# Windowed attention with two feed-forward layers on one core: one polynomial step gets a choice of engine, and the order of all work is found anew

## The chip, the core and the metric

The kernel runs on one core of a Trainium2 chip. The metric is the time of one execution on the device in microseconds. Before the change it was run three times, with a median of 931.73 us (930.45 to 932.07).

A core has engines that work at the same time, each through its own queue and strictly in that queue's order: TensorE (PE) multiplies matrices, VectorE (DVE) and GpSimd (POOL) do elementwise work, ScalarE (ACT) computes `func(scale * x + bias)`, and SyncE (SP) issues the DMAs. An engine whose next instruction waits does nothing else in the meantime. Results of TensorE lie in PSUM, everything else in SBUF.

## What is computed

Three stages run one after the other. Everything is float32.

```python
scores = scale * np.matmul(q, k.transpose(0, 1, 3, 2))      # 4 batches, 8 heads, 576 positions, 64 wide
scores = np.where(mask, scores + bias[None], -1000000000.0)  # window of 128, slopes by head
attn = softmax(scores);  x = np.matmul(attn, v)              # then 2304 tokens x 512

h = x @ w_in                                                 # layer 1: 512 -> 2048
P = a[0] + a[1]*h + a[2]*h*h + a[3]*h*h*h
Q = 1.0 + np.abs(b[0])*np.abs(h) + np.abs(b[1])*h*h
x = (P / (Q + 1e-06)) @ w_out                                # 2048 -> 512

r = np.maximum(x @ w2_in, 0.0)                               # layer 2: 512 -> 2048
out = (r * r) @ w2_out                                       # 2048 -> 512
```

The denominator Q is evaluated by Horner's scheme from `ah = |h|`: the first step is `t = |b1| * ah + |b0|`, the second `t = t * ah`, and the 1 is added in the logarithm that follows.

## The kernel before

**Stages and tiles.** Attention works on 16 pairs of heads. Layer 1 runs over five blocks of tokens, numbered 0 to 4 (512 tokens each, block 1 has 256). In a block there are 16 steps `f`, one for each 128 of the 2048 hidden columns. A step first computes `h` with 12 matmuls (`gemm_in`, L758; the planner's name is `g1`), then passes `h` through a chain on the other engines, and then adds its part to the block's output with 12 more matmuls (`gemm_out`, L843, `g2`). Each operand is split into a high and a low half (`xh`/`xl`, `gh`/`gl`, weights `hi`/`lo`), and three products are summed. Layer 2 runs over blocks 5 to 8 of 512 tokens in two pairs, and a last block 9 of 256. In the pairs the first product is done by Strassen's scheme: block 5 or 7 computes for each of eight `r` the products m1, m2, m6, m7 and m4 (L907, 6 matmuls each), with a `g2` before m7 and one before m4 once the first `r` is through. Blocks 6 and 8 reuse saved products and need only m5 and m3. Block 9 is computed plainly.

**The chain of a step in layer 1.** `r_abs` (ACT, L771) makes `ah`; `r_u` (ACT, L775) and `r_p` 1 and 2 (DVE, L791 and L793) make the numerator; `r_t` 1 (POOL, L783) and `r_t` 2 (POOL, L785) make the denominator; `r_r` 1 and 2 (ACT, L799 and L801, a logarithm and an exponential) its reciprocal; `r_g` 1 to 3 (DVE, L811) a correction of it and the quotient. Then `gh` (ACT, L230) and `gl` (DVE, L237) split the result for `g2`. There are four PSUM banks for `h`, so `g1` of a step waits until `gl` of the step four before it is done.

**Work beside the chain.** The weights come as float64 in 64 chunks of 512 KB (`wl`, L207) and are turned to float32 on the chip: `w0` (ACT, POOL or DVE), `w1`, `w2`, `w3` (DVE, L222, L224, L226), `w4` (ACT or POOL) and `w5` (POOL or DVE, L237). For Strassen's scheme sums of the second layer's weights (`wS`, L251, then `sh` and `sl`) are made while layer 1 runs, written to DRAM, and read back as `wc` (`wcl`, L887, six buffers). Sums of the layer's input are made as well (`xrraw`, L866, then `xh` and `xl`). In blocks 5 and 7 the products m1, m6, m7 and m4 all leave the same PSUM bank one after the other, so each is copied away first (`keep`, L333 on ACT and L335 on DVE; the planner's names are c1, c6, c7 and c4): m6 waits for c1, m7 for c6, m4 for c7.

**What sets the order.** All work is entered in a `Plan` with its predecessors, the engines that may do it, a duration for each, and a priority. The priority is the place in the computation plus a constant for the kind of work from the table `BIAS`. `Plan.run` then goes through the work while the program is built: among everything whose predecessors are placed it takes the piece that can start first, the priority deciding between equal starts, and among an operation's engines the one with the smallest key. The order in which pieces are placed becomes the order of every engine's queue. The durations are written in the `plan.add` calls, so they influence the order but nothing that the chip does.

Of the kernel before, what the change touches and what calls it, by code (L numbers as in the profile page):

```python
# [11 lines left out]
AF = mybir.ActivationFunctionType  # L12
ALU = mybir.AluOpType


class Plan:
# [30 lines left out]
    def run(self):  # L47
# [10 lines left out]
        while ready:  # L58
            best = None
            for name in ready:  # L60
                _, after, prio, engs, _, port = self.ops[name]
                for eng, cost in engs.items():
# [14 lines left out]
                    key = (t + WEIGHT * prio, prio, t + cost)  # L77
# [26 lines left out]
BIAS = {'m1': 176.6, 'm2': -67.7, 'm5': 149.1, 'm6': 127.0, 'm7': 157.7, 'm4': 44.6, 'm3': 130.0, 'c1': -700.0, 'c6': -650.8, 'c7': -700.0, 'r1': -1260.2, 'r2': -907.1, 'r3': -822.4, 'c4': -868.5, 'W0': -855.7, 'W1': -753.0, 'W2': -251.8, 'W3': -1053.3, 'attn_end': -383.7, 'bias': -208.2, 'exp': 197.5, 'g1': 149.1, 'g2': 156.4, 'gh': 19.1, 'gl': -1269.8, 'ldk': -606.3, 'ldk0': 90.7, 'ldq': -386.7, 'ldq0': 1045.6, 'ldr': 233.1, 'ldv': 438.3, 'plus': -298.8, 'ptc': -864.9, 'ptp': 27.1, 'pv': -205.6, 'r_abs': 504.7, 'r_g1': -42.9, 'r_g2': -440.7, 'r_g3': -622.6, 'r_p1': -62.7, 'r_p2': 498.8, 'r_r1': 5.2, 'r_r2': -13.6, 'r_t1': 138.0, 'r_t2': 443.3, 'r_u': 515.3, 'rcp': 512.1, 'rout': -71.4, 'rtc': -143.4, 'rtp': 322.1, 's': -77.1, 's_g': 464.4, 's_relu': 107.1, 'scl': 343.4, 'scp': 258.8, 'trk': 302.8, 'trk0': -480.7, 'trk0c': -71.0, 'trkc': -657.2, 'trq': 307.2, 'trq0': -470.2, 'trq0c': 124.1, 'trqc': -120.9, 'trr': 153.9, 'trrc': -273.4, 'ttr': -969.4, 'w0': 1271.0, 'w1': 133.2, 'w2': 38.4, 'w3': -221.6, 'w4': 912.4, 'w5': -244.0, 'warm': -84.2, 'wl': -225.2, 'x': 240.5, 'xh': -109.1, 'xl': -304.1, 'xld': 93.6, 'xn': 493.8, 'xo': 50.4, 'xr': -44.7, 'yc': 96.0, 'yo': -594.2, 'sq': -681.2, 'd1': -167.3, 'sh': -77.4, 'wS': 582.4, 'd4': -185.5, 'wo': 15.5, 'd5': -249.0, 'wpl': -0.4, 'd2': -0.2, 'd3': 0.6, 'so': 315.5, 'sl': -57.0}  # L104
WEIGHT = 0.0000
# [7 lines left out]
def tile_window_attention_moe_moe(  # L113
# [854 lines left out]
    for n, (nme, f) in enumerate(CHUNKS):  # L968
# [65 lines left out]
    def gate(ji, f, pr, last, free=()):  # L1034
# [18 lines left out]
    def prep(ji, i):  # L1053
# [18 lines left out]
        def diff(name, dst, a, b, after):  # L1072
            plan.add(
                (name, ji, i), lambda eng: x_diff(eng, k0(dst), k0(a), k0(b)), DVE=0.6, Pool=1.23, after=after, prio=p0 - 8, port=True
            )

        def halves(k, q, after):
# [3 lines left out]
            else:  # L1081
# [3 lines left out]
                ("xl", ji, k, i), lambda eng: x_half(eng, ji, k, i, k0(q), "xl"), DVE=0.6, Pool=1.23, after=[op] + fl, prio=p0 - 7, port=True  # L1085
# [17 lines left out]
    def pair(ji, r):  # L1103
# [83 lines left out]
    for ji, (kind, t0, n) in enumerate(jobs):  # L1187
# [40 lines left out]
        for f in range(NF):  # L1228
# [18 lines left out]
            if kind == "a":  # L1247
                op("r_abs", r_abs, ["g1"], 1, [("r_r2", *prev(2))], ACT=(0.26, 0.48))
                op("r_u", r_u, ["r_abs"], 1.2, [("r_g3", *prev(3))], ACT=(0.45, 0.66))
                op("r_t", r_t, ["r_abs"], 1.5, [("r_g2", *prev(2))], 1, Pool=(0.54, 0.72))  # L1250
                op("r_t", r_t, ["r_t1"], 1.7, (), 2, Pool=(0.69, 1.23))
                op("r_p", r_p, ["r_u"], 2, (), 1, DVE=(0.33, 0.6))
                op("r_p", r_p, ["r_p1"], 2.2, (), 2, DVE=(0.4, 0.66))
                op("r_r", r_r, ["r_t2"], 3, (), 1, ACT=(0.4, 0.62))
                op("r_r", r_r, ["r_r1", "r_p2"], 3.2, (), 2, ACT=(0.31, 0.52))
                op("r_g", r_g, ["r_r2"], 4, (), 1, DVE=(0.33, 0.6))
                op("r_g", r_g, ["r_g1"], 4.2, (), 2, DVE=(0.33, 0.6))
                op("r_g", r_g, ["r_g2", "r_p2"], 4.4, (), 3, DVE=(0.4, 0.66))
                last = "r_g3"
            else:  # L1260
# [58 lines left out]
```

## Time and profile before

| | us |
|---|---|
| median of three runs | 931.73 |
| lowest, highest | 930.45, 932.07 |
| the profiled execution | 934.74 |
| its span, first to last instruction | 933.0 |
| PE busy in the span | 905.1 |
| DVE, ACT, POOL busy | 671.7, 506.0, 423.2 |

The profile is that of one execution, and its own time lies 3.0 us above the median of the runs. Layer 1 starts at 141 us, when attention is nearly done, and goes on until about 555 us, the two pairs of Strassen blocks until about 879 us, and the last block until the end. An engine's busy time counts its instructions and no waits. In the lists of groups and the timelines an instruction is named by its source line and its tiles, with the buffer's number left out. A wait is put down to the work that ended last before the instruction started.

### The profile page before, as it was taken

To read this page: it belongs to the slowest core of one execution; us is meant where nothing else is said; L and a number is where in the kernel's file an instruction comes from. 1 tells how busy PE (TensorE), PEld (TensorE's weight loads), DVE (VectorE), ACT (ScalarE), POOL (GpSimd) and SP (SyncE) were. 2 spreads that over 40 slices of the span, in tenths; PEclk is the share of its full clock that TensorE was granted. 3 is DMA by queue.
4 is the path that set the end of the run, shared out by engine and by line. 5 is a ranking of instruction groups with operands and counts; after the bars stand their busy time and mean duration, and the time that the engine had idled before them with its cause. 6 is when DMAs were issued, how large, how long until landed. Compare 5 with 4: busy or idle time off the path is not lost.

```text
span 933.0 us, 14472 instructions
## 1 busy us (share of the span) xinstructions
PE 905.1 (97%) x4812; PEld 743.7 (80%) x4812; DVE 671.7 (72%) x1304; ACT 506.0 (54%) x1111; POOL 423.2 (45%) x441
## 2 busy tenths in 40 slices
PE   8989999999999999999999698999999999999998
PEld 6667767888998888888788576888888888888897
DVE  4898798999788998988899997942674432255432
ACT  4879987766657666766664754432331432221232
POOL 4355347788367878777779832400340200000100
PEclk9999999999999999999999899999999999999999
DMA  7999974321324633543254558633532734692010
GB/s 169 239 250 229 228 216 130 103 75 43 103 58 136 180 117 110 176 140 113 91 169 137 169 159 306 225 104 111 169 102 69 226 106 123 199 335 94 1 46 23
DMA packets 137482, 134.73 MB, mean 144 GB/s; under 512 B 68144, under 2 KB 99776, under 8 KB 137408
## 3 DMA queue, kind: packets, MB, share of 16 engines
q1 hardware_dynamic: 137408, 133.81, 48.1%
q8 instruction: 38, 0.62, 0.3%
q14 instruction: 36, 0.29, 0.1%
HBM read 102.76 MB, written 31.01 MB: 143 GB/s over the span
## 4 chain that ended last, share of the span: by engine, by line
PE 43%; POOL 4%; DVE 3%; issue 1%; DMA 1%; ACT 0%; POOLq 0%; DVEq 0%
PE y L843 23%; PE ps L907 16%; PE h L758 4%; POOL xrraw L866 1%; POOL xl L237 1%; DMA wc<-wsum 1%; POOL t L783 1%; POOL t L785 1%; DVE h L811 0%; DVE t L811 0%; POOL ws L251 0%; DVE u L793 0%; DVE u L791 0%; DVE gl L237 0%; DVE win2r L222 0%
## 5 line engine op out<-in xcount | busy, mean ns | idle before, releaser
L907 PE MATMUL ps<-xh,wc 128*128 128x512 f32 x448 | 149.0, 391 | 4.2 <-DMA wc<-wsum 3.5
L758 PE MATMUL h<-xh,win1hi 128*128 128x512 f32 (+1 forms) x320 | 119.1, 372 | 8.6 <-DVE gl L237 8.6
L758 PE MATMUL h<-xl,win1hi 128*128 128x512 f32 (+1 forms) x320 | 118.4, 370 | 0.0
L758 PE MATMUL h<-xh,win1lo 128*128 128x512 f32 (+1 forms) x320 | 118.3, 370 | 0.0
L843 PE MATMUL y<-gh,wout1hi 128*128 128x512 f32 (+1 forms) x320 | 117.8, 368 | 0.0
L843 PE MATMUL y<-gl,wout1hi 128*128 128x512 f32 (+1 forms) x320 | 117.8, 368 | 0.0
L843 PE MATMUL y<-gh,wout1lo 128*128 128x512 f32 (+1 forms) x320 | 117.8, 368 | 0.0
L843 PE MATMUL y<-wout2hi,gl 128*128 128x512 f32 x288 | 112.8, 392 | 0.0
L843 PE MATMUL y<-wout2hi,gh 128*128 128x512 f32 x288 | 112.8, 392 | 0.0
L843 PE MATMUL y<-wout2lo,gh 128*128 128x512 f32 x288 | 112.6, 391 | 0.0
L785 POOL TENSOR_TENSOR t<-t,ah 128x512 f32<-128x512 f32 (+1 forms) x80 | 100.3, 1256 | 5.0
L907 PEld LDWEIGHTS ps<-xh,wc 128*128 128x128 f32 x448 | 84.2, 188 | 22.5 <-DMA wc<-wsum 3.9
L939 DVE SCALAR_TENSOR_TENSOR ah<-ah 128x512 f32<-128x512 f32 x64 | 48.9, 764 | 66.5 <-ACT ah L333 64.9
L230 ACT ACTIVATE gh<-ah 128x512 fp32r<-128x512 f32 x64 | 40.3, 629 | 100.0 <-DVE ah L939 100.0
L783 POOL TENSOR_SCALAR t<-ah,ab_sb 128x512 f32<-128x512 f32 (+1 forms) x80 | 66.8, 835 | 52.8 <-ACT ah L771 30.4
L907 PE MATMUL ps<-xl,wc 128*128 128x512 f32 x224 | 87.5, 391 | 0.0
L230 ACT ACTIVATE gh<-h 128x512 fp32r<-128x512 f32 (+1 forms) x96 | 50.1, 522 | 53.0 <-PE y L843 35.2
L237 DVE TENSOR_TENSOR gl<-ah,gh 128x512 fp32r<-128x512 f32 x64 | 45.9, 718 | 43.4 <-ACT gh L230 43.2
L799 ACT ACTIVATE ah<-t,one_eps 128x512 f32<-128x512 f32 (+1 forms) x80 | 54.4, 680 | 41.8 <-POOL t L785 41.0
L758 PEld LDWEIGHTS h<-xh,win1hi 128*128 128x128 f32 x320 | 60.7, 190 | 20.0 <-DVE gl L237 9.9
L454 ACT ACTIVATE e<-e,st 128x256 f32<-128x256 f32 (+1 forms) x144 | 66.9, 467 | 8.3 <-DVE st L438 8.2
L237 DVE TENSOR_TENSOR gl<-h,gh 128x512 fp32r<-128x512 f32 (+1 forms) x96 | 57.3, 597 | 18.6 <-ACT gh L230 18.2
(152 smaller groups left out, 2061.0 us busy)
## 6 DMA issues: line engine op xcount, KB each, us to landing
wc<-wsum SPq DMA_DIRECT2D x64, 256.0 KB, 3.7
wc<-wp SPq DMA_DIRECT2D x48, 256.0 KB, 3.5
win1r<-in_moe_w_in_dram SPq DMA_DIRECT2D x16, 512.0 KB, 4.5
wout1r<-in_moe_w_out_dram SPq DMA_DIRECT2D x16, 512.0 KB, 3.3
win2r<-in_moe_w_in_dram SPq DMA_DIRECT2D x16, 512.0 KB, 4.7
wout2r<-in_moe_w_out_dram SPq DMA_DIRECT2D x16, 512.0 KB, 3.2
xrraw<-ys SPq DMA_DIRECT2D x44, 128.0 KB, 3.5
xs<-xT SPq DMA_DIRECT2D x16, 288.0 KB, 3.7
```

Of the source, the lines that this page charges most:

```text
L230: nc.scalar.activation(dst, src, AF.Copy)
L237: (nc.vector if eng == "DVE" else nc.gpsimd).tensor_tensor(dst, a, b, ALU.subtract)
L454: nc.scalar.activation(e, e, AF.Exp, scale=-1.0, bias=s[:, j : j + 1], accum_out=sums[p % 3][:, c : c + 1],)
L758: nc.tensor.matmul(h[:, :n], a[:, c * P : (c + 1) * P], bb[:, :n], start=(m == 0), stop=(m == 3 * NCC - 1),)
L783: nc.gpsimd.tensor_scalar(gt("t", 2, ji, f), ah, ab_sb[:, 1:2], ab_sb[:, 0:1], ALU.mult, ALU.add)
L785: nc.gpsimd.tensor_tensor(tl["t", ji, f], tl["t", ji, f], ah, ALU.mult)
L799: nc.scalar.activation(ah, tl["t", ji, f], AF.Ln, bias=one_eps)
L843: nc.tensor.matmul(dst, a, bb, start=(first and m == 0), stop=(last and m == 2))
L866: (nc.vector if eng == "DVE" else nc.gpsimd).tensor_tensor(tl[dst], tl[a], tl[b], ALU.subtract)
L907: nc.tensor.matmul(dst, w, x, start=(k in (1, 2, 5) and m == 0), stop=(m == 5), skip_group_check=True)
L939: nc.vector.scalar_tensor_tensor(t, t, 0.0, t, ALU.max, ALU.mult)
```

## The change

There are three parts, in one diff.

1. The first Horner step of the denominator becomes an operation of its own, `r_t1`, which ScalarE may do as well as GpSimd; the planner chooses. On ScalarE it is `Identity(scale * ah + bias)` with the two coefficients as columns of 128. The second step stays on GpSimd under the name `r_t2`.
2. Durations in the planner are replaced by longer ones, for the chain of layer 1, the copies c1 to c4, the sums and halves of the inputs, and the bits of the weights from layer 1's output matrix on.
3. The table `BIAS` has new numbers for 55 of its 96 kinds (one of them, `wcl`, is new), and the sort key loses the term `WEIGHT * prio`, which was zero, and gains `HOLD`, an offset in us for a kind on an engine. A negative number makes that engine more likely to be taken for that kind.

```diff
-                    key = (t + WEIGHT * prio, prio, t + cost)
+                    key = (t + HOLD.get((name[0], eng), 0.0), prio, t + cost)
...
-WEIGHT = 0.0000
+HOLD = {('r_u', 'ACT'): 0.14, ('d5', 'Pool'): 0.16, ('c4', 'DVE'): -1.0, ('d5', 'DVE'): -0.15, ('c6', 'DVE'): -1.0, ('rcp', 'DVE'): 0.03, ('w0', 'DVE'): 0.01, ('c7', 'DVE'): -0.12, ('trq0c', 'DVE'): 0.02, ('xn', 'Pool'): -0.33, ('r_abs', 'ACT'): 0.01, ('trk', 'PE'): 0.01, ('trk0', 'PE'): 0.98, ('rtc', 'DVE'): 0.3, ('w4', 'Pool'): 0.04}
...
-    def r_t(ji, f, k):
-
-        ah = tl["ah", ji, f]
-        if k == 1:
-            nc.gpsimd.tensor_scalar(gt("t", 2, ji, f), ah, ab_sb[:, 1:2], ab_sb[:, 0:1], ALU.mult, ALU.add)
-        else:
-            nc.gpsimd.tensor_tensor(tl["t", ji, f], tl["t", ji, f], ah, ALU.mult)
+    def r_t1(eng, ji, f):
+        t, ah = gt("t", 2, ji, f), tl["ah", ji, f]
+        if eng == "ACT":
+            nc.scalar.activation(t, ah, AF.Identity, bias=ab_sb[:, 0:1], scale=ab_sb[:, 1:2])
+        else:
+            nc.gpsimd.tensor_scalar(t, ah, ab_sb[:, 1:2], ab_sb[:, 0:1], ALU.mult, ALU.add)
+
+    def r_t2(ji, f):
+        nc.gpsimd.tensor_tensor(tl["t", ji, f], tl["t", ji, f], tl["ah", ji, f], ALU.mult)
...
-                ("xl", ji, k, i), lambda eng: x_half(eng, ji, k, i, k0(q), "xl"), DVE=0.6, Pool=1.23, after=[op] + fl, prio=p0 - 7, port=True
+                ("xl", ji, k, i), lambda eng: x_half(eng, ji, k, i, k0(q), "xl"), DVE=0.8, Pool=1.45, after=[op] + fl, prio=p0 - 7, port=True
...
-            plan.add(op, lambda eng: keep(eng, ji, r, k), ACT=0.48, DVE=0.6, after=[name({1: 1, 6: 6, 7: 7, 4: 4}[k])] + after, prio=pr)
+            plan.add(op, lambda eng: keep(eng, ji, r, k), ACT=0.58, DVE=0.68, after=[name({1: 1, 6: 6, 7: 7, 4: 4}[k])] + after, prio=pr)
...
-                op("r_t", r_t, ["r_abs"], 1.5, [("r_g2", *prev(2))], 1, Pool=(0.54, 0.72))
-                op("r_t", r_t, ["r_t1"], 1.7, (), 2, Pool=(0.69, 1.23))
+                op("r_t1", r_t1, ["r_abs"], 1.5, [("r_g2", *prev(2))], Pool=(0.56, 0.9), ACT=(0.55, 0.77))
+                op("r_t2", r_t2, ["r_t1"], 1.7, (), Pool=(0.72, 1.33))
```

Built, the planner puts 58 of the 80 first steps on ScalarE and leaves 22 on GpSimd. The number of matmuls is the same. In blocks 5 to 8 nearly all copies c4, c6 and c7 go to VectorE, 47 more than before.

**The place where TensorE waits longest, VectorE's queue.** It is the end of block 4, from `gl` of step 8 on. In the names `h4_9` is block 4, step 9, and the last number only tells buffers apart. L811 and L791/L793 (L813 and L793/L795 after the change) are the chain of layer 1; `wb`, `win2r`, `wout2r` are weights being converted, `ws`/`wsl` their sums, and `xl5`/`xrraw_5` inputs of block 5. Before:

```order
L237 TENSOR_TENSOR gl4_8_6359<-h4_8_6167,gh4_8_6354 128x512
L251 TENSOR_TENSOR ws6_1_6269<-wb44_5914,ws6_0_6268 128x256
L217 TENSOR_SCALAR wb46_6380<-win2r_14_6212 128x512
L237 TENSOR_TENSOR wsl6_1_6390<-ws6_1_6269,wsh6_1_6366 128x512
L224 SCALAR_TENSOR_TENSOR wb46_6380<-wb46_6380,win2r_14_6212 128x512
L226 SCALAR_TENSOR_TENSOR wb46_6380<-win2r_14_6212,wb46_6380 128x512
L237 TENSOR_TENSOR win2lo_14_6432<-wb46_6380,win2hi_14_6418 128x512
L237 TENSOR_TENSOR xl5_4_1_6440<-xrraw_5_1_2_6286,xh5_4_1_6434 128x512
L222 TENSOR_SCALAR win2r_15_6382<-win2r_15_6382 128x512
L222 TENSOR_SCALAR wout2r_0_6416<-wout2r_0_6416 128x512
L224 SCALAR_TENSOR_TENSOR wb47_6413<-wb47_6413,win2r_15_6382 128x512
L811 SCALAR_TENSOR_TENSOR t4_9_6283<-t4_9_6283,h4_9_6228 128x512
```

Seven more instructions follow before `gl` of step 9. In the changed kernel the same stretch of the same queue is this, complete:

```order
L237 TENSOR_TENSOR gl4_8_6358<-h4_8_6143,gh4_8_6353 128x512
L795 SCALAR_TENSOR_TENSOR u4_10_6314<-u4_10_6314,ca_sb_112,h4_10_6256 128x512
L813 SCALAR_TENSOR_TENSOR t4_9_6281<-t4_9_6281,h4_9_6228 128x512
L813 SCALAR_TENSOR_TENSOR h4_9_6228<-t4_9_6281,h4_9_6228 128x512
L813 SCALAR_TENSOR_TENSOR t4_10_6333<-t4_10_6333,h4_10_6256 128x512
L813 SCALAR_TENSOR_TENSOR h4_9_6228<-u4_9_6303,ca_sb_112,h4_9_6228 128x512
L813 SCALAR_TENSOR_TENSOR h4_10_6256<-t4_10_6333,h4_10_6256 128x512
L813 SCALAR_TENSOR_TENSOR h4_10_6256<-u4_10_6314,ca_sb_112,h4_10_6256 128x512
L251 TENSOR_TENSOR ws6_1_6296<-wb44_5911,ws6_0_6295 128x256
L222 TENSOR_SCALAR win2r_15_6378<-win2r_15_6378 128x512
L237 TENSOR_TENSOR gl4_9_6444<-h4_9_6228,gh4_9_6437 128x512
```

Of the ten conversions and sums in a row, two are left between the two `gl`; the others stand earlier, later or on GpSimd.

**SyncE's queue at the change from block 4 to block 5.** `wc5_1_3` is the fourth part of the weights that block 5 needs for its second `r`, `ys` the output of block 4, and `wout2r` a chunk of raw weights. Before:

```order
L887 DMA wc5_1_1_6780<-wp2_120 128x512
L887 DMA wc5_1_2_6783<-wsum1_135 128x512
L207 DMA wout2r_5_6799<-in_moe2_w_out_dram 128x1024
L856 DMA ys1792_185<-yt4_0_6820 128x512
L207 DMA wout2r_6_6830<-in_moe2_w_out_dram 128x1024
L856 DMA ys1792_185<-yt4_1_6823 128x512
L856 DMA ys1792_185<-yt4_2_6828 128x512
L856 DMA ys1792_185<-yt4_3_6834 128x512
L887 DMA wc5_1_3_6855<-wsum1_135 128x512
```

And in the changed kernel:

```order
L889 DMA wc5_1_1_6759<-wp2_120 128x512
L889 DMA wc5_1_2_6761<-wsum1_135 128x512
L889 DMA wc5_1_3_6791<-wsum1_135 128x512
L889 DMA wc5_1_4_6795<-wp3_121 128x2x256
L207 DMA wout2r_4_6799<-in_moe2_w_out_dram 128x1024
L858 DMA ys1792_185<-yt4_0_6811 128x512
L889 DMA wc5_2_0_6828<-wp4_122 128x512
```

The load of `wc5_1_3` no longer stands behind two chunks of weights and the four writes of block 4's output.

On TensorE's queue the order of blocks 5 to 8 stays as it was, but for one place: the last `g2` of block 4 (of step 15) stood between m6 and m7 of block 5's first `r` and now stands between m7 and m4. In blocks 2 to 4 `g1` and `g2` mostly come in twos (two steps' `g1`, then two steps' `g2`) where they alternated.

## Rows read from the trace of the kernel before

**Rows 1.** The page: span, and busy time by engine.

```profile
span 933.0 us, 14472 instructions
PE 905.1 (97%) x4812; PEld 743.7 (80%) x4812; DVE 671.7 (72%) x1304; ACT 506.0 (54%) x1111; POOL 423.2 (45%) x441
```

**Rows 2.** TensorE's waits: us in total, times, longest.

```profile
PE h L758 <- DVE gl L237: 8.6, 3, 7.2
PE ps L907 <- DMA wc<-wsum: 3.5, 1, 3.5
PE ps L907 <- DVE U L335: 0.8, 1, 0.8
```

**Rows 3.** Windows: mean length, busy us (instructions) by engine, clock, DMA share, GB/s.

```profile
0.00:150.00 150.00, 139.08 (x1159) 100.94 (x1160) 117.22 (x434) 122.44 (x419) 72.66 (x106) 1.00 0.88 215
150.00:460.00 310.00, 309.13 (x1570) 262.74 (x1569) 282.11 (x477) 211.34 (x389) 231.34 (x232) 1.00 0.36 114
460.00:470.00 10.00, 9.04 (x40) 7.19 (x39) 10.00 (x17) 8.27 (x14) 6.13 (x6) 1.00 0.03 11
480.00:520.00 40.00, 35.23 (x156) 28.83 (x154) 38.80 (x48) 21.36 (x37) 36.87 (x31) 0.98 0.38 126
520.00:530.00 10.00, 7.60 (x27) 6.20 (x28) 9.45 (x15) 7.27 (x13) 10.00 (x12) 0.73 0.44 154
560.00:570.00 10.00, 6.54 (x22) 4.97 (x21) 6.35 (x12) 4.76 (x8) 0.00 (x0) 0.83 1.02 364
```

**Rows 4.** Timeline of VectorE, 503 to 522 us: start, length, instruction.

```profile
503.74 0.68 DVE L237 TENSOR_TENSOR gl<-h,gh 128x512 fp32r<-128x512 f32 x1
504.35 0.91 DVE L251 TENSOR_TENSOR ws<-wb,ws 128x256 f32<-128x256 f32 x1
...
507.63 1.77 DVE L224 SCALAR_TENSOR_TENSOR wb<-wb,win2r 128x512 int32<-128x512 int32 x1
...
516.76 0.68 DVE L224 SCALAR_TENSOR_TENSOR wb<-wb,win2r 128x512 int32<-128x512 int32 x1
...
521.67 0.68 DVE L237 TENSOR_TENSOR gl<-h,gh 128x512 fp32r<-128x512 f32 x1
```

**Rows 5.** Timeline of GpSimd, 505 to 517 us.

```profile
505.81 4.74 POOL L237 TENSOR_TENSOR xl<-xrraw,xh 128x512 fp32r<-128x512 f32 x3
510.51 1.74 POOL L866 TENSOR_TENSOR xrraw<-xrraw,xrraw 128x512 f32<-128x512 f32 x1
512.25 1.21 POOL L783 TENSOR_SCALAR t<-ah,ab_sb 128x512 f32<-128x512 f32 x1
513.42 3.13 POOL L785 TENSOR_TENSOR t<-t,ah 128x512 f32<-128x512 f32 x2
```

**Rows 6.** The chain of waits, 522 to 573 us: start, length, what.

```profile
522.40 4.43 PE h L758 x12
526.84 2.72 PE y L843 x12
...
556.80 0.70 DVE U L335
...
557.54 1.42 PE ps L907 x5
558.96 6.87 DMA wc<-wsum
...
565.87 1.64 PE ps L907 x4
567.51 3.90 PE y L843 x12
```

**Rows 7.** Groups by shape, whole span: busy us, mean ns, idle before.

```profile
L783 POOL TENSOR_SCALAR t<-ah,ab_sb 128x512 f32<-128x512 f32 x64 | 57.9, 904 | 35.1 <-ACT ah L771 12.9 <-DVE h L811 12.0 <-ACT u L775 4.0
L775 ACT ACTIVATE u<-h,na_sb 128x512 f32<-128x512 f32 x64 | 49.4, 772 | 0.8 <-DVE h L811 0.8
L335 DVE COPY U<-ps 128x512 f32<-128x512 f32 x2 | 1.4, 682 | 0.3 <-PE ps L907 0.3
```

More of the change, by code (lines that the diff above doesn't have):

```diff
@@ L988, in tile_window_attention_moe_moe @@
         )
-        plan.add(("w1", n), lambda n=n: w_bits(n, 1), DVE=0.34, after=[("wl", n)], prio=pr + 0.3, port=True)
-        plan.add(("w2", n), lambda n=n: w_bits(n, 2), DVE=0.6, after=[("w0", n), ("w1", n)], prio=pr + 0.6, port=True)
-        plan.add(("w3", n), lambda n=n: w_bits(n, 3), DVE=0.6, after=[("w2", n)], prio=pr + 1.2, port=True)
+        plan.add(("w1", n), lambda n=n: w_bits(n, 1), DVE=0.34 if lst == 0 else 0.52, after=[("wl", n)], prio=pr + 0.3, port=True)
+        plan.add(("w2", n), lambda n=n: w_bits(n, 2), DVE=0.6 if lst == 0 else 0.75, after=[("w0", n), ("w1", n)], prio=pr + 0.6, port=True)
+        plan.add(("w3", n), lambda n=n: w_bits(n, 3), DVE=0.6 if lst == 0 else 0.75, after=[("w2", n)], prio=pr + 1.2, port=True)
         plan.add(
@@ L1037, in gate @@
         plan.add(
-            ("sq", ji, f), lambda: square(ji, f), DVE=0.6, after=[last], prio=pr + 3, port=True
+            ("sq", ji, f), lambda: square(ji, f), DVE=0.75, after=[last], prio=pr + 3, port=True
         )
         plan.add(
-            ("gh", ji, f), lambda: g_hi(ji, f), ACT=0.52, after=[("sq", ji, f), ("g2", *p3), ("gh", *p1)], prio=pr + 5
+            ("gh", ji, f), lambda: g_hi(ji, f), ACT=0.61, after=[("sq", ji, f), ("g2", *p3), ("gh", *p1)], prio=pr + 5
         )
         plan.add(
-            ("gl", ji, f), lambda: g_lo(ji, f), DVE=0.6, after=[("gh", ji, f), ("g2", *p3), ("gl", *p1)], prio=pr + 6, port=True
+            ("gl", ji, f), lambda: g_lo(ji, f), DVE=0.71, after=[("gh", ji, f), ("g2", *p3), ("gl", *p1)], prio=pr + 6, port=True
         )
@@ L1073, in diff @@
             plan.add(
-                (name, ji, i), lambda eng: x_diff(eng, k0(dst), k0(a), k0(b)), DVE=0.6, Pool=1.23, after=after, prio=p0 - 8, port=True
+                (name, ji, i), lambda eng: x_diff(eng, k0(dst), k0(a), k0(b)), DVE=0.7, Pool=1.4, after=after, prio=p0 - 8, port=True
             )
@@ L1123, in save @@
             op = (f"c{k}", ji, r)
-            plan.add(op, lambda eng: keep(eng, ji, r, k), ACT=0.48, DVE=0.6, after=[name({1: 1, 6: 6, 7: 7, 4: 4}[k])] + after, prio=pr)
+            plan.add(op, lambda eng: keep(eng, ji, r, k), ACT=0.58, DVE=0.68, after=[name({1: 1, 6: 6, 7: 7, 4: 4}[k])] + after, prio=pr)
         def add(k, after):
-            plan.add((f"r{k}", ji, r), lambda: join(ji, r, k), DVE=0.6, after=after, prio=pr)
+            plan.add((f"r{k}", ji, r), lambda: join(ji, r, k), DVE=0.68, after=after, prio=pr)
         g = [("g2", *steps[ji * NF + 2 * r - 2 + j]) for j in range(2)]
@@ L1263, in tile_window_attention_moe_moe @@
                 last = "s_g"
[L1264 to L1265 removed]
+            op("gh", g_hi, [last], 5, [("g2", *prev(3)), ("ptp", NU - 1)], ACT=(0.36, 0.57))
+            op("gl", g_lo, ["gh"], 6, [("g2", *prev(3))], DVE=(0.41, 0.68))
             after = [("gl", ji, f), ("w5", wid["wout1" if kind == "a" else "wout2", f]), ("g2", *prev(1))]
```

22 lines of the change are left out of this document (10 added, 12 removed).

## The prediction, made before the changed kernel was run

> **What bounds the kernel now.** The first view is the page. TensorE is busy for 905.1 of the 933.0 us [rows 1], and the change neither adds nor removes a matmul. So whatever it gains must come from the 27.9 us in which TensorE is idle, or from stretches in which its matmuls ran slowly, and the reader should look for those two things only.
>
> The second view is the list of TensorE's waits, and the third the windows that say where they lie [rows 2, 3]. The first 150 us, nearly all attention, have 150 - 139.08 = 10.9 us of idle TensorE in many small pieces. From there to 460 us it is idle for only 0.9 us of 310. Then come four visible waits: about 1 us in 460 to 470 us, and three others that can be named. One wait of 7.2 us for `gl` is the largest in the kernel [rows 2]. A wait of 0.8 us for a copy and one of 3.5 us for a load of `wc` come 35 to 45 us later. The output behind the last matmul holds nearly all the rest, and the change leaves it alone.
>
> The chain of waits shows that the long waits cost more than their length [rows 6]. Twelve matmuls that take 2.72 us at full speed took 4.43 us right behind the 7.2 us wait, so 1.71 us were lost again. Behind the wait for `wc` four matmuls took 1.64 us where a third of 2.72, 0.91, is usual (0.73 lost), and the next twelve took 3.90 (1.18 lost). The granted clock of these two stretches is 0.73 and 0.83 where it is 1.00 elsewhere [rows 3]: part of each ran at the lower of the two levels, 1.2 GHz instead of 2.4, after TensorE had stood still.
>
> Next is the reason for the 7.2 us. VectorE's timeline between two `gl` shows ten instructions in a row that have nothing to do with the waiting chain, from the sum at 504.35 to the weight conversion that ends at 517.36 [rows 4]. They took 13.0 us, although one of them alone takes 0.68 where nothing disturbs it (the one at 516.76); the same instruction took 1.77 us at 507.63. GpSimd meanwhile worked through three `xl` and a sum, and only then, at 512.25, came to the first Horner step of the waiting chain, and to two second steps behind it [rows 5]. In 480 to 520 us VectorE was busy for 38.8 of 40 us and GpSimd for 36.9, ScalarE for 21.4 [rows 3]. The two engines that the chain shares with the preparation of block 5 were full, and the third one was half free.
>
> **The change part by part.**
>
> *First Horner step to ScalarE.* 58 of 80 leave GpSimd, of these 13 of 16 in block 4. One costs GpSimd 904 ns; the nearest row for it on ScalarE is `r_u`, the same function with the same kind of operands at 772 ns [rows 7]. In block 4 GpSimd is relieved of 13 x 0.90 = 11.7 us and ScalarE gets 13 x 0.77 = 10.0 us, over about 87 us of TensorE's work (32 pieces of 2.72 us [rows 6]). ScalarE was busy for 211 of 310 us in blocks 0 to 3 [rows 3]; with about 45 x 0.77 = 35 us more it stands at 246 of 310, below TensorE. So what it adds is hidden, and it becomes the bound only if its queue is badly ordered.
>
> One rule speaks against this part. The Trainium skill, "ScalarE: Activation LUTs", section "Rules for kernel authors", says to put multiplications and additions on VectorE and not on ScalarE. No row here shows this step on VectorE. Were it there, the 58 steps would join the queue that was busy for 38.8 of 40 us, and at the 0.68 us of its shortest row above they would add 39 us to it; so the row decides, and the sum goes by ScalarE.
>
> *The new order, end of block 4.* Between `gl` of steps 8 and 9 VectorE's queue holds two foreign instructions instead of ten in a row. By the lone duration they are about 1.3 us instead of 13.0, so the 7.2 us wait goes: 7.17 + 1.71 = 8.9 us removed. What is late next is `gl` of step 11, for which `g1` of step 15 must wait. Between `gl` of 10 and of 11 the new queue has 16 instructions, 11 of the chain and five weight conversions. TensorE has four pieces there, 4 x 2.72 = 10.9 us. Undisturbed, 16 x 0.68 = 10.9 us, which just fits; if the four long conversions take 1.77 us each, as at 507.63, it is 4 x 1.09 = 4.4 us too late. I take 2.5 us, slightly more than half, because GpSimd has eight two-operand instructions in a row at that time. That is a residual wait between 0 and 4.4.
>
> *The wait in 460 to 470 us* has the same form (`h` waits for `gl` of block 4's first step), 1.0 us. In the old queue of GpSimd three sums or halves stood between the first and second Horner step there, in the new one none: 1.0 removed.
>
> *Change from block 4 to 5.* Together 3.5 + 0.8 + 0.73 + 1.18 = 6.2 us are lost there. The load of the fourth part of `wc` needs the buffer that m7 frees. The copy behind m7 started at 556.80, so m7 had ended; the load was issued at 558.96, behind the writes of block 4's output, and landed 6.87 us later [rows 6]. In the new queue of SyncE it stands ahead of them, which is worth 2.2 us, and `g2` of step 15 now lies behind m7, which gives another 2.72 us of cover: 4.9 against a wait of 3.5. So that wait goes, with the slow matmuls behind it. I keep 0.5 us (0 to 2, if the loads that are now issued close together share the bandwidth). In exchange m7 follows m6 directly and must wait for the copy c6, as m4 waited for c7: 0.8 us by that wait [rows 2], up to 1.5 if the copy stands behind another instruction. I take 1.0. The old 0.8 for c7 is covered by `g2` now.
>
> *Copies on VectorE.* 47 copies of 682 ns, 32 us, go from ScalarE to VectorE in blocks 5 and 7. Each pair of steps there takes 5 x 1.36 + 2 x 2.72 = 12.2 us of TensorE, and VectorE has about 15 instructions in it: 10.2 us. A copy of c6 or c7 has the 2.72 us of a `g2` to hide in. I cost them at nothing; what happens without that cover is the rival below.
>
> *Everything else.* The order of attention is new too, with the same operations and durations. Nothing in the rows says whether its 10.9 us of idle time grow or shrink; I take 0, with 5 either way (half of it). For blocks 0 to 3 with their 0.9 us I add 1.0, one more wait like the one at 460 us (0 to 3). The longer durations in the planner cost nothing by themselves.
>
> *Sum.* Removed: 8.9 + 1.0 + 6.2 = 16.1. Given back: 2.5 + 0.5 + 1.0 + 1.0 = 5.0. Net -11.1 us. The profiled execution took 934.7 us (span 933.0 and 1.7 around it), so it would take 923.6. The median of the runs is 931.73, 3.0 us below; the same difference brings **920.6 us**.
>
> **The rivals.**
>
> *The stall moves.* The chain's waits are shifted rather than removed: `gl` of 11 comes the full 4.4 us late, TensorE drops to the lower clock again and loses 1.7 there too, c6 costs 1.5, `wc` 2, blocks 0 to 3 give 3. Given back is then 12.6 instead of 5.0: -3.5, or 928. For it speaks that VectorE stays nearly full there; against it that its queue between the gates has lost foreign work. 925 to 930 us.
>
> *A larger gain.* No residual waits, and attention gives up to 5 us as well: -16 to -21, or 911 to 916. For it: the search could order attention anew with an added offset; against it: nothing in the rows of attention names a single long wait that an order could take away.
>
> *No change.* TensorE waits elsewhere for as much as it gains, for instance on ScalarE, where in-order queueing puts a `r_u` or `r_t1` of a later step ahead of a reciprocal that is due. 930 to 933.6.
>
> *Slower.* Mechanism: the copies c6 and c7 on VectorE. There are about 31 of them in blocks 5 and 7. m7 and m4 wait for them; before, TensorE waited once for a copy in all of these blocks [rows 2]. A copy takes 0.68 of the 2.72 us of cover, so 2.0 us remain for what stands ahead of it on VectorE, one undisturbed instruction or one that is disturbed as at 507.63, but not two. Late by 0.36 us on the average, they eat the 11.1 us; late by 0.8, that is 25 us, it is 945. Against it: in the order the copies stand right behind instructions that are ready early. 934 to 945.
>
> That the change does not do what it says is excluded, since 58 of 80 steps stand on ScalarE's queue.
>
> **How the numbers follow.** Chances: forecast (916 to 925) 0.50; the stall moves 0.15; larger gain 0.14; no change 0.08; slower 0.13. A measurement of this kernel tells 0.2% from no change, 1.9 us, so faster means below 929.9: 0.50 + 0.15 + 0.14 = 0.79. Same is 0.08, slower 0.13. The range takes in the first three and half of the fourth case, 911 to 931, and leaves out the slower case and a little more.
>
> **What would show it.** Right: no wait of TensorE for `gl` above 3 us in block 4, no granted clock below 0.9 in 500 to 570 us, no wait for `wc` over 2 us, a new wait of about 1 us for a copy c6 between m6 and m7, and ScalarE up and GpSimd down by some 45 us. Wrong: TensorE waiting for copies in blocks 5 and 7 (slower), a `gl` wait of 5 us or more (the stall moves), or attention's idle time off 10.9 by more than 5 us.

## The result, and the profile of the changed kernel

The changed kernel takes **923.4 us** (median; 922.45 to 923.97) beside 931.9 for the kernel before on the same chip: a ratio of 0.9909, 95% interval 0.9892 to 0.9927, so about 8.5 us faster. Forecast were 920.6 us and a range of 911 to 931. A second comparison with more runs (below) gave 0.9891 (0.9871 to 0.9912), about 10 us.

The page, the same two lines as [rows 1]:

```profile
span 920.6 us, 14425 instructions
PE 903.6 (98%) x4812; PEld 742.6 (81%) x4812; DVE 671.9 (73%) x1334; ACT 523.5 (57%) x1146; POOL 368.9 (40%) x376
```

TensorE's idle time fell from 27.9 to 17.0 us. ScalarE gained 17.5 us: 45 us of first steps came, and the copies that went to VectorE left (43 of them; four of the 47 that stand there now stood there before). GpSimd lost 54.

TensorE's waits, to be held against [rows 2] (us in total, times, longest):

```profile
PE tr L387 <- ACT qkT L333: 1.6, 4, 0.5
PE s L427 <- DVE qkT L335: 1.6, 2, 0.8
...
PE ps L909 <- DVE U L335: 0.8, 1, 0.8
...
PE h L758 <- DVE gl L237: 0.5, 1, 0.5
```

The waits of 7.2 us for `gl` and of 3.5 us for `wc` are gone. What heads the list now is attention; its largest single wait for `qkT` is 0.8 us here, and 2.2 in the second profile below.

The windows of [rows 3] (mean length, busy us and instructions of PE, PEld, DVE, ACT, POOL, clock, DMA share, GB/s):

```profile
0.00:150.00 150.00, 139.52 (x1151) 100.02 (x1152) 120.00 (x441) 121.43 (x421) 71.44 (x103) 1.00 0.91 222
150.00:460.00 310.00, 308.59 (x1567) 262.52 (x1566) 271.34 (x468) 240.70 (x441) 193.58 (x190) 1.00 0.35 110
460.00:470.00 10.00, 10.00 (x45) 8.26 (x44) 9.05 (x16) 7.70 (x13) 5.14 (x5) 1.00 0.21 80
480.00:520.00 40.00, 40.00 (x177) 32.94 (x176) 36.19 (x53) 32.73 (x57) 33.42 (x25) 1.00 0.31 102
520.00:530.00 10.00, 10.00 (x45) 8.27 (x45) 9.24 (x16) 7.98 (x14) 9.11 (x9) 1.00 0.75 236
560.00:570.00 10.00, 10.00 (x46) 8.12 (x45) 7.28 (x10) 3.59 (x6) 5.09 (x3) 1.00 0.93 325
```

In the four short windows from 460 us on TensorE is busy without a gap and the clock is 1.00, where it was down to 0.73 and 0.83.

VectorE's timeline between `gl` of steps 8 and 9, as [rows 4] (start, length):

```profile
503.76 0.68 DVE L237 TENSOR_TENSOR gl<-h,gh 128x512 fp32r<-128x512 f32 x1
...
508.98 1.54 DVE L251 TENSOR_TENSOR ws<-wb,ws 128x256 f32<-128x256 f32 x1
510.44 1.52 DVE L222 TENSOR_SCALAR win2r<-win2r 128x512 int32<-128x512 int32 x1
511.88 0.68 DVE L237 TENSOR_TENSOR gl<-h,gh 128x512 fp32r<-128x512 f32 x1
```

`gl` of step 9 starts at 511.88, where it started at 521.67.

The chain of waits at the change to block 5, as [rows 6] (start, length, what):

```profile
541.06 4.09 PE ps L909 x18
...
545.17 0.70 DVE U L335
...
545.92 1.66 PE ps L909 x6
```

Here m7 follows m6 and waits for the copy c6: the one wait that is left there.

### The profile page after: what moved, and what is told of

Its sections match the earlier page's. It is cut to its first block, busy times and chain, and to the rows that moved or that the text cites. A ratio compares the mean times of both kernels' runs of the same rounds, so it can differ in the third digit from the quotient of the medians.

```text
span 920.6 us, 14425 instructions
## 1 busy us (share of the span) xinstructions
PE 903.6 (98%) x4812; PEld 742.6 (81%) x4812; DVE 671.9 (73%) x1334; ACT 523.5 (57%) x1146; POOL 368.9 (40%) x376
## 4 chain that ended last, share of the span: by engine, by line
PE 91%; DVE 4%; ACT 3%; issue 1%; POOL 1%; POOLq 0%; ACTq 0%; DVEq 0%
PE y L845 43%; PE h L758 23%; PE ps L909 17%; PE pt L491 2%; PE o L517 2%; ACT e L454 2%; PE s L427 1%; DVE e L438 1%; PE tr L387 1%; PE warm L670 1%; ACT xT L333 0%; ACT qkT L333 0%; ACT ptsb L333 0%; DVE wb L224 0%; DVE wb L226 0%
## 5 line engine op out<-in xcount | busy, mean ns | idle before, releaser
L787 POOL TENSOR_TENSOR t<-t,ah 128x512 f32<-128x512 f32 (+1 forms) x80 | 97.4, 1218 | 65.4 <-ACT t L782 55.1
L771 ACT ACTIVATE ah<-h 128x512 f32<-128x512 f32 (+1 forms) x80 | 44.1, 552 | 45.6 <-PE h L758 45.1
L758 PEld LDWEIGHTS h<-xh,win1hi 128*128 128x128 f32 x320 | 60.3, 189 | 11.2 <-DVE gl L237 1.0
L845 PEld LDWEIGHTS y<-gh,wout1lo 128*128 128x128 f32 x320 | 60.4, 189 | 10.0
L758 PEld LDWEIGHTS h<-xh,win1lo 128*128 128x128 f32 x320 | 60.3, 188 | 10.0
```

Source lines behind the costliest of these rows:

```text
L758: nc.tensor.matmul(h[:, :n], a[:, c * P : (c + 1) * P], bb[:, :n], start=(m == 0), stop=(m == 3 * NCC - 1),)
L771: nc.scalar.activation(gt("ah", 2, ji, f), tl["h", ji, f], AF.Abs)
L787: nc.gpsimd.tensor_tensor(tl["t", ji, f], tl["t", ji, f], tl["ah", ji, f], ALU.mult)
L845: nc.tensor.matmul(dst, a, bb, start=(first and m == 0), stop=(last and m == 2))
```

## The experiments

In all of these kernels the planner's search is replaced by a list of steps and engines that was written out beforehand, and the experiment is an edit of that list. The code of the steps is the changed kernel's, so its line numbers hold (the first Horner step is L782 on ScalarE and L784 on GpSimd).

```diff
-                    key = (t + HOLD.get((name[0], eng), 0.0), prio, t + cost)
+        order = json.loads(zlib.decompress(base64.b64decode(ORDER)))
+        for name, eng in order:
```

One table serves all runs. It is worked out from the starts of TensorE's matmuls in each trace: the time of a marked matmul less 0.227 us for each matmul of 512 columns (0.120 for 256) of the two layers that started before it. What is left up to the last matmul of attention is attention's own time; what is added between later marks was lost in waits or at the lower clock. The marks are the last `g2` matmul of block 3, the last `g2` matmul of block 4, and a place in block 5 behind both. TensorE takes up the first steps of block 4 ahead of the first mark, so the wait in 460 to 470 us counts there; and where m7 stands ahead of the last `g2` of block 4, the wait for c6 lies ahead of the second mark. All in us.

| run | attention | blocks 0 to 3 | block 4 | change to 5 | median | kernel before, same runs |
|---|---|---|---|---|---|---|
| kernel before, profile of before | 145.4 | 1.9 | 8.9 | 6.5 | 931.9 | |
| changed kernel, first profile | 148.0 | 0.6 | 1.2 | 0.0 | 923.4 | 931.9 |
| rb_before_again | 143.2 | 2.0 | 10.0 | 7.3 | 933.8 | 934.6 |
| ra_after_again | 148.8 | 0.6 | 1.1 | 0.0 | 923.6 | 934.6 |
| e1_gpsimd_only | 148.3 | 1.4 | 2.8 | 0.0 | 924.9 | 934.6 |
| e2_scalar_old_order | 143.8 | 13.3 | 10.2 | 6.3 | 945.7 | 934.6 |
| e3_vector_row | 142.9 | 2.0 | 20.5 | 7.4 | 944.6 | 933.2 |
| e5_three_queues | 143.0 | 2.1 | 20.3 | 7.6 | 944.5 | 933.2 |
| e4_block_change | 143.0 | 2.0 | 11.2 | 3.9 | 930.8 | 933.2 |
| e45_both_repairs | 144.3 | 1.8 | 21.1 | 3.0 | 942.5 | 933.2 |
| h4_new_from_block4 | 143.0 | 2.4 | 1.1 | 0.0 | 919.5 | 933.9 |
| h4x_old_from_block4 | 148.7 | 0.6 | 9.5 | 6.3 | 937.5 | 933.9 |
| e6_copies_scalar | 148.3 | 0.6 | 1.0 | 0.0 | 923.7 | 933.9 |
| h1_old_attention | 143.8 | 10.3 | 1.1 | 0.0 | 926.9 | 932.5 |

Behind the change to block 5 all runs are alike within 1 us.

### Both kernels once more

> The kernel before once more, with its order of work written out as a list, so that a second profile of the same instructions in the same queues exists. The first profile lay 2.8 us above the median of its runs. If the stalls at 510 to 525 and 563 to 571 us vary from run to run, this profile shows them at another length and its own time is nearer to 931.9 (wait for gl between 4 and 7 us, less time at the lower clock). If they are fixed and something else made that profile longer, the same 7.2 and 3.5 us stand there again. The timed ratio to the kernel before should be 1.000 within 0.002.

> The changed kernel once more, its order written out as a list; the base for the runs beside it. Expected 923.4, ratio 0.991. If the changed kernel has no long stall that can vary, its profile shows the same as the first: no wait of TensorE above 1.6 us before 880 us, and a time within 1 us of the median.

The kernel before came to 0.9995 (0.9982 to 1.0008) of itself, so the list does what the search did. The stalls are no chance; the second profile's list of TensorE's waits has them again:

```profile
PE h L758 <- DVE gl L237: 8.6, 3, 7.1
PE ps L909 <- DMA wc<-wsum: 3.3, 1, 3.3
```

Two things varied. Attention took 143.2 us where the first profile has 145.4. And the same wait for `gl` cost more behind it, since more of the next twelve matmuls ran at the lower clock: 5.49 us, where [rows 6] has 4.43 and full speed is 2.72.

```profile
520.16 5.49 PE h L758 x12
```

The median of the kernel before was 934.6 over 15 runs, 933.2 over 13, 933.9 over 13 and 932.5 over 11 in the four later comparisons, on three chips. So the three runs shown ahead of the prediction lay at the low end, and its profile was not out of the ordinary. The changed kernel stayed at 923.55. Of its profile a wait of at most 1.6 us was expected, and one in attention is 2.2.

### The choice of engine alone

```diff
-r_t1.4_9 ACT
+r_t1.4_9 Pool
...
```

> The changed kernel's order with all 80 first Horner steps back on GpSimd, nothing else moved: the choice of engine undone alone. Theory A (the order removed the stalls; the engine matters little): 923.5 to 926, no wait for gl above 2 us. Theory B (the order only works because ScalarE takes the first step): GpSimd gets 58 x 0.9 = 52 us more, in block 4 11.7 us, its first and second steps come late and TensorE waits for gl in block 4 for 5 us or more in all: 929 to 940.

All 80 first steps are back on GpSimd, in the changed kernel's order. The ratio is 0.9906 (0.9885 to 0.9926) where the changed kernel has 0.9891 beside it: theory A. TensorE's waits between 140 and 600 us:

```profile
PE h L758 <- DVE gl L237: 2.5, 3, 1.5
```

By the table the choice is worth 0.8 us in blocks 0 to 3 and 1.7 in block 4. By the medians it is 1.3 in all, and the two intervals overlap, so an effect of the choice in this order is not clear of noise.

```diff
 r_abs.4_9 ACT
+r_t1.4_9 ACT
...
-r_t1.4_9 Pool
```

> The order of the kernel before, with the same 58 first Horner steps on ScalarE that the changed kernel has there, each put on ScalarE's queue right behind its absolute value (as far as its buffer allows): the choice of engine alone. If the 7.2 us wait comes from GpSimd being late alone, it shrinks by 3 us or more: 925 to 929. If VectorE's ten foreign instructions in a row hold gl as well, the wait stays within 1.5 us of the old one, and the time is 930 to 934. The change from block 4 to 5 should look as before in both (3.5 us for wc).

In the old order the same choice, with the step right behind the absolute value, makes the kernel *slower*, 1.0118 (1.0086 to 1.015), 11 us, which by the table lie in blocks 0 to 3. Both theories had missed this. The first line is TensorE's waits over the whole span, the second ScalarE's waits from 140 to 560 us, the third the same of the changed kernel (second profile):

```profile
PE h L758 <- DVE gl L237: 13.4, 10, 6.6
```

```profile
ACT t L782 <- DVE h L813: 14.2, 15, 1.5
```

```profile
ACT t L782 <- DVE h L813: 2.6, 4, 1.0
```

There are two buffers for `t`, so a first step waits until VectorE has finished `r_g2` two steps earlier. On GpSimd that wait held GpSimd; on ScalarE, right behind the absolute value, it holds everything that ScalarE has to do for the chain. In the changed kernel's order the first steps stand where the buffer is mostly free. That this wait makes up the 11 us is argued from the two lists; no run put the step at another place of the old order. The wait of 7 us in block 4 stayed at 6.6.

### The long wait in block 4

```diff
 gl.4_8 DVE
-wS.6_4 DVE
-w0.46 DVE
...
 gl.4_10 DVE
+wS.6_4 DVE
+w0.46 DVE
...
```

> The order of the kernel before with one thing moved: the ten foreign instructions between gl of steps 8 and 9 of block 4 on VectorE (with what depends on them) stand behind gl of step 10. No change of engine. Theory A (the prediction's: VectorE's row alone holds gl of step 9): the 7.2 us wait and its 1.7 us of slow matmuls go, the time is 8.9 lower, 925 to 927 beside 934 for the kernel before, no wait for gl above 3 us. Theory B (three queues are late at once; GpSimd's second step of the chain ends at 515 and ScalarE's at 515 too): 1 to 3 us at most, 931 to 933, and a wait for gl of 4 us or more stays in 505 to 525 us.

The ten instructions, an eleventh (`w3.47`) and the 13 steps that depend on them, among these the loads of two more chunks, stand behind `gl` of step 10. The ratio is 1.0131 (1.0112 to 1.0151): both theories wrong in the time. The first wait shrank only from 7.1 to 5.2 us, which is theory B's size. VectorE's timeline, then ScalarE's and GpSimd's; the bracket is the idle time before an instruction and what ended it:

```profile
512.55 0.69 DVE L813 SCALAR_TENSOR_TENSOR t<-t,h 128x512 f32<-128x512 f32 x1 [9.90 <-ACT h L803]
```

```profile
506.65 0.67 ACT L214 ACTIVATE wb<-win2r 128x512 f32<-128x512 f32 x1 [4.49 <-DMA win2r<-in_moe_w_in_dram]
509.06 0.63 ACT L230 ACTIVATE xh<-xrraw 128x512 fp32r<-128x512 f32 x1 [1.74 <-POOL xrraw L868]
511.08 0.72 ACT L801 ACTIVATE ah<-t,one_eps 128x512 f32<-128x512 f32 x1 [1.38 <-POOL t L787]
...
534.71 0.68 ACT L214 ACTIVATE wb<-wout2r 128x512 f32<-128x512 f32 x1 [9.30 <-DMA wout2r<-in_moe_w_out_dram]
```

```profile
504.00 3.79 POOL L237 TENSOR_TENSOR xl<-xrraw,xh 128x512 fp32r<-128x512 f32 x3
```

In the profile of before the row was not what came last either. ScalarE's reciprocal for this step, which had waited for GpSimd's second step, ended at 516.53, and VectorE took up the chain at 517.36, so the row itself kept the chain from starting there by 0.8 us:

```profile
515.17 0.72 ACT L799 ACTIVATE ah<-t,one_eps 128x512 f32<-128x512 f32 x1 [2.25 <-POOL t L785]
515.93 0.60 ACT L801 ACTIVATE h<-ah 128x512 f32<-128x512 f32 x1
```

With its row free, VectorE stood idle for 9.9 us: the reciprocal that it needs came late from ScalarE, which had waited for a load, for a sum by GpSimd and for GpSimd's second step. Then came the price, a new wait of TensorE of 11.0 us. SyncE's waits from 495 to 545 us, its timeline and VectorE's show where it begins:

```profile
SPq L262 <- ACT wsh L230: 22.4, 2, 19.8
```

```profile
524.82 0.38 SPq L207 DMA_DIRECT2D wout2r<-in_moe_w_out_dram  x1
...
530.88 0.33 SPq L207 DMA_DIRECT2D wout2r<-in_moe_w_out_dram  x1
```

```profile
524.04 0.69 DVE L226 SCALAR_TENSOR_TENSOR wb<-win2r,wb 128x512 int32<-128x512 int32 x1
...
530.16 0.69 DVE L226 SCALAR_TENSOR_TENSOR wb<-win2r,wb 128x512 int32<-128x512 int32 x1
```

The moved work was not foreign to the chain. A chunk of raw weights is loaded into the buffer that `w3` of the chunk two before sets free, and SyncE takes these loads and the writes of sums in one queue. The queue stood for 19.8 us at the write of a sum whose half had been moved behind, the next chunk was asked for at 524.82 and the one after it at 530.88, each right after the `w3` that frees its buffer, and ScalarE waited 9.3 us for them with the absolute value of the chain's next step behind that in its queue. In the profile of before the same two loads were issued at these times:

```profile
511.13 0.33 SPq L207 DMA_DIRECT2D wout2r<-in_moe_w_out_dram  x1
...
518.66 0.33 SPq L207 DMA_DIRECT2D wout2r<-in_moe_w_out_dram  x1
```

The next edit comes on top of that one:

```diff
-xh.5_4_1 ACT
...
 gl.4_10 DVE
+xh.5_4_1 ACT
...
 r_t1.4_9 Pool
+r_t2.4_9 Pool
 xl.5_1_1 Pool
...
+r_t1.4_10 Pool
+r_t2.4_10 Pool
 wS.6_3 Pool
```

> As the run with VectorE's row moved, and besides the half of the input that ScalarE waited for ahead of its logarithm of step 9 is moved behind too, and on GpSimd the Horner steps of steps 9 and 10 stand ahead of the three halves and the sum. All first Horner steps are still on GpSimd. Theory B: the 7.2 us wait and the 1.7 us go, or a smaller wait of up to 2 us appears at a later gl: 925 to 927.5. Theory C (without ScalarE taking the first step GpSimd is too full for any order): a wait of 4 us or more appears at a later gl: 929 to 934.

1.0127 (1.0109 to 1.0146), outside both expected ranges. With GpSimd's steps ahead as well, the first wait shrinks further, to 3.0 us and 1.3 at the `gl` before, 4.3 in all. What ScalarE then waits for ahead of the reciprocal is a load again:

```profile
510.04 0.67 ACT L214 ACTIVATE wb<-win2r 128x512 f32<-128x512 f32 x1 [4.50 <-DMA win2r<-in_moe_w_in_dram]
```

The later wait is 13.3 us long. So VectorE's was not the only late queue (theory B on the cause), though 4.3 of the 7 us are left with all three changed; and moving conversions behind starves the loads. That it is GpSimd's fullness (theory C) the run does not show, since the later wait has the cause seen in the run before.

### The change from block 4 to block 5

```diff
-g2.4_15 PE
 m7.5_0 PE
+g2.4_15 PE
...
+wcl.5_1_3 SP
+wcl.5_1_4 SP
 wl.53 SP
 yo.4_0 SP
...
```

> The order of the kernel before with only the change from block 4 to block 5 repaired: on TensorE m7 of block 5's first r stands ahead of the last gemm_out of block 4, on SyncE the loads of the fourth and fifth part of wc stand ahead of the writes of block 4's output. By the prediction's sum: 6.2 removed, 0.5 to 1.0 given back at copy c6, so 5.2 to 5.7 lower than the kernel before, 928 to 929 beside 934; the 7.2 us wait for gl stays. If the early loads share bandwidth with the writes and come no earlier: 2.7 to 3.5 lower only, and a wait for wc stays.

0.9976 (0.9963 to 0.9989), 2.3 us instead of 5.2 to 5.7. The wait for `wc` and the lower clock are gone, as forecast: 1.00 in every window from 530 to 580 us. In their place TensorE waits 3.7 us for copies (540 to 600 us):

```profile
PE ps L909 <- ACT U L333: 1.9, 2, 1.2
PE ps L909 <- ACT ah L333: 1.2, 1, 1.2
PE ps L909 <- DVE U L335: 0.6, 1, 0.6
```

The copies stand behind weight conversions on ScalarE, and those, by way of VectorE's, behind loads: ahead of the wait of 1.2 us for `ah` ScalarE had waited 2.15 us for VectorE's `w3`, and VectorE 2.08 us for a chunk. In the old kernel the wait for `wc` lay over this stretch.

```diff
+the edit of e5_three_queues
+the edit of e4_block_change
```

> Both repairs of the old order together, with every first Horner step still on GpSimd and everything else as before. If the changed kernel's gain is these two places and nothing else, this gains as much or more than it, since attention keeps its old order: the two gains add to 13 to 14.6, 920 to 921.5 beside 934, no time at the lower clock before 900 us. If the choice of engine is needed for it, 924 to 929, with a wait for gl in block 4 of 3 us or more.

The two edits together give 1.0105 (1.0084 to 1.0126), outside both expected ranges. The table has both effects side by side, 21.1 us lost in block 4 and 3.0 at the change; they add up, and no gain comes of it.

### Which stretch of the new order matters

```diff
 steps of the old order up to g1.4_0
-steps of the old order from g1.4_0
+steps of the changed kernel's order from g1.4_0
```

> The order and engines of the kernel before up to the first gemm_in of block 4 (attention and blocks 0 to 3), and the changed kernel's order and engines from there. Theory A (the gain lies in block 4 and the change to block 5 alone, and attention's new order costs about 2.6 us): block 4 gives 7.7 and the change to block 5 gives 6.5, so 14 lower than the kernel before, 919 to 921, below the changed kernel. Theory B (the new order of blocks 0 to 3 prepares block 4, by conversions done earlier): a wait for gl of 3 us or more stays in block 4, 924 to 929.

919.45 us, a ratio of **0.9854** (0.983 to 0.9877), the fastest kernel here and theory A's number. The longest wait of TensorE behind attention is 1.5 us, at the seam. Two windows, as above:

```profile
500.00:530.00 30.00, 30.00 (x134) 24.84 (x133) 29.43 (x42) 25.34 (x44) 25.12 (x23) 1.00 0.41 141
560.00:580.00 20.00, 19.63 (x87) 15.92 (x86) 14.41 (x21) 8.59 (x15) 9.60 (x7) 1.00 0.69 222
```

```diff
 steps of the changed kernel's order up to g1.4_0
-steps of the changed kernel's order from g1.4_0
+steps of the old order from g1.4_0
```

> The mirror image: the changed kernel's order and engines up to the first gemm_in of block 4, the old ones from there. Theory A: both old stalls are back (7 us for gl, 3.5 us for wc, and the lower clock behind each), the time is that of the kernel before plus what attention's order costs less 1.3 for blocks 0 to 3: 933 to 937. Theory B: the old stalls shrink, 925 to 930.

The mirror image gives 1.0038 (1.0016 to 1.0061), 937.5 us, with both old waits:

```profile
PE h L758 <- DVE gl L237: 8.0, 2, 7.4
...
PE ps L909 <- DMA wc<-wsum: 3.4, 1, 3.4
```

At the cut the two orders differ in eight steps only, so block 4 starts from almost the same state in both. The gain is what the queues do from there, and what stands ahead of it costs some 4 us (919.5 against 923.6, and 937.5 against 933.9). It is attention that costs: with the old one (nine runs, 142.9 to 145.4, median 143.2) against the new one (five runs, 148.0 to 148.8, median 148.3) it is about 5 us longer.

```diff
+steps of the old order up to g1.0_4
-steps of the changed kernel's order up to g1.0_4
 steps of the changed kernel's order from g1.0_4
```

> The kernel before's order and engines for attention (up to the fifth gemm_in of block 0), the changed kernel's from there on. By the stages of the runs so far, attention ends at about 143 us in the old order and at 148 to 149 in the new one, and blocks 0 to 3 with the start of block 4 lose about 2 us to waits in the old order and 0.6 in the new. If attention's order alone is the loss: 5 lower than the changed kernel and 1.3 lower than the run that keeps the old order up to block 4, 918 to 919. If the new order of blocks 0 to 3 depends on the new attention (tiles that are ready earlier), a wait of 1 to 4 us appears in block 0, and the time is 920 to 923.

0.9932 (0.9918 to 0.9945), slower than both expected ranges: the old attention is as short as ever, but at this seam blocks 0 to 3 lose nearly 10 us more than in the changed kernel, all of it in block 0. TensorE's waits, then the chain of waits:

```profile
PE h L758 <- DVE gl L237: 6.9, 2, 6.4
```

```profile
159.69 3.71 DMA wout1r<-in_moe_w_out_dram
...
163.49 0.43 DVE wout1r L222
163.92 0.60 DVE h L813
```

VectorE's next instruction is a conversion of a chunk that has not landed, and the chain stands behind it. It is the same loop of raw weights as in block 4.

### Copies

```diff
-c6.5_0 DVE
+c6.5_0 ACT
...
```

> The changed kernel with the copies c4, c6 and c7 back on ScalarE, the order otherwise kept. If the copies' engine matters little, as the prediction had it: within 0.5 us of the changed kernel's 923.5, with the wait for c6 still 0.8. If copies on ScalarE stand behind weight conversions that wait for their DMA, as in the run with the change of blocks repaired in the old order (3.7 us of waits for copies there): 925 to 928, with waits of TensorE for a copy of U or ah on ScalarE of 1 us or more between 545 and 575 us.

923.65 beside 923.55: the engine of the copies does not matter. The waits for copies, 540 to 600 us:

```profile
PE ps L909 <- ACT U L333: 0.7, 1, 0.7
PE ps L909 <- ACT ah L333: 0.2, 1, 0.2
```

So it is not VectorE that saved the copies from the 3.7 us above. What is left is the new order; that it is the place of the conversions in it is argued, since no run moved them alone.

## Why the prediction came out as it did

The difference came out right in size. The sum said 11.1 us less. The span falls by 12.4 from the first profile of before to the first of after and by 11.3 from the second to the second; the medians differ by 8.5 in the first comparison, with four runs each, and by 11.0 in the larger one. **The absolute time** was 2.8 us too low, because the sum was hung on a median of three runs. The sentence "the same difference brings 920.6" is the step that failed; against a median of 934 the same sum gives 923. The time of the kernel before moves by 2 us with its mean granted clock (last section), which three runs do not settle.

Term by term:

- *Block 4*, 8.9 removed and 2.5 given back: net 6.4 forecast. Lost there were 8.9 and 10.0 in the two profiles before, 1.2 and 1.1 after, and nearly all of that, 0.95, is c6. The residual wait for `gl` of step 11 did not come: TensorE does not wait for `gl` in block 4 at all.
- *The wait in 460 to 470 us*, 1.0: gone, as forecast.
- *Change to block 5*, 6.2 removed, 0.5 kept for `wc`, 1.0 for c6: removed 6.5 and 7.3, no wait for `wc`, and at c6 a wait of 0.8 us that cost 0.95, the same that is counted above.
- *Blocks 0 to 3*, 1.0 more waiting: 0.7 before and 0.7 after up to the last step of block 3, so nothing.
- *Attention*, 0 with 5 either way: 2.6 lost from the first profile to the first, 5.6 from the second to the second, 5 by the medians of all runs, the very edge of that bound. The terms above were together 4.4 and 6.5 us too cautious, and attention took it back: that the sum is right is luck, since two errors met.
- *Copies on VectorE*, 0, and the rival that made them 25 us: 0, and with the copies back on ScalarE 0 again. 43 copies moved, not 47.

Of the signs named, the waits, the clock and c6 came as said. ScalarE rose by 17.5 us and not by 45, because the copies that the prediction itself took off it had been left out of that sign. And the sign for attention, its idle time, did not come although attention grew.

**The reason given for the 7.2 us was only a part of it.** The prediction named VectorE's ten instructions, and gave the wait as gone with them. Taking just these away brought 2 us of 7 and cost 11 later, because they feed the loop that loads raw weights. GpSimd's late first step, which it also read [rows 5], released the chain, by way of ScalarE's reciprocal, only 0.8 us before VectorE's row did. ScalarE, which it called half free, was the next to be late: in the run with all three queues changed its reciprocal came out behind a wait of 4.5 us for a load. It had 21 us of work in 40, and in an in-order queue a wait for a load blocks the chain's instructions behind it; a busy share does not show that.

**ScalarE as the free engine**, the feature that the change is named for, is worth 1.3 us by the medians in the new order, which is not clear of noise, and as it was placed here costs 11 in the old. The Trainium skill's rule weighed in the prediction ("ScalarE: Activation LUTs", "Rules for kernel authors": additions and multiplications on VectorE) stays undecided, since no run put this step on VectorE. The time per step was well sized from [rows 7], 0.77 taken from `r_u`, 0.81 measured:

```profile
L782 ACT ACTIVATE t<-ah,ab_sb 128x512 f32<-128x512 f32 x48 | 38.9, 812 | 2.9 <-DVE h L813 1.9
```

Open is whether the search would have found such an order with the choice forbidden (the runs undo the choice in the order that it found), and which of the durations, `BIAS` and `HOLD` led it there. Open is also why the new attention is 5 us longer. In the first 160 us TensorE is idle for 11.3 and 11.4 us in the first profiles of before and after, and for 9.0 and 12.8 in the second ones, so waits are only a part of it; the rest are matmuls that follow each other more slowly, and no run takes the two apart.

## What to carry to other kernels

Work that stands between two steps of a waiting chain is foreign only if nothing that feeds the chain's queues depends on it; follow the buffer that it frees to the load that waits for it before calling its removal a gain. The stall here, at which several in-order queues were late together, was not mended by moving work on one of them or on three, while a new order of all queues from one seam on removed it. Such a stretch is the unit to try, and parts of a new order that don't pay, here attention, can be kept out of it. A forecast of a difference should be stated against the middle of as many runs as there are: here three runs of the kernel before lay 0.7 to 2.9 us below the medians of 11 to 15 runs.

## What the runs showed of the hardware

*VectorE beside GpSimd.* The three `xl` took 4.74 us on GpSimd while VectorE worked [rows 5] and 3.79 in the run where VectorE stood idle, and a VectorE instruction of 0.68 us alone took 1.77 beside GpSimd [rows 4]: 1.09 more, a little less than one `xl` alone (3.79 / 3 = 1.26). The Trainium skill, "SBUF — State Buffer", section "Who interferes with whom", says that a port pair which the two engines share is an exclusive lock, and that a VectorE instruction with two inputs in SBUF contends with a GpSimd instruction that reads SBUF. These lengths agree with that. Both queues thus ran slower where they were fullest.

*The clock behind a wait.* Twelve matmuls of 2.72 us at full speed took 4.43 behind the wait of 7.2 us [rows 6], and the chain of waits of the run with VectorE's row moved has this behind its wait of 11.0:

```profile
539.64 4.56 PE h L758 x12
544.21 13.62 PE y L845 x60
```

So 1.84 us are lost, and the next sixty run at full speed. Behind the shorter wait of 6.4 us in h1_old_attention 24 matmuls took 8.06 us where 5.44 is usual, 2.6 lost:

```profile
167.69 8.06 PE h L758 x24
175.75 2.72 PE y L845 x12
```

The loss does not follow the length of the wait: behind the waits of 7.2 and 7.1 us in the two profiles of before the same twelve matmuls lost 1.71 and 2.77. In the changed kernel, with no wait above 0.8 us behind attention, the clock was 1.00 in every window shown.

*Spread.* Runs of the kernel before lay between 930.5 and 938.5 us, those of the changed kernel between 922.1 and 925.4. Of the 52 runs of the kernel before in the later comparisons, the 22 with a mean granted clock of 0.992 or less have a median of 934.7 us, the 30 others 932.6; all runs of the changed kernel have 0.996 or more. The two profiles of before, at 0.994 and 0.990, differ behind the two long waits: 3.6 and 5.6 us were lost there at the lower clock. For the other runs that this is the reason is argued.
